# Unit 2's p in f16 by transposing transfers, unit 3 normalised on ScalarE, first loads by pair of heads, and a new order of all queues

## The chip, the cores and the metric

One core of a Trainium2 chip runs the kernel. The metric is the device time of one execution in microseconds (us). Matrix products run on TensorE (PE; its weight loads are PEld), elementwise work and reductions on VectorE (DVE), activations, copies and conversions on ScalarE (ACT), and SyncE (SP) issues nearly all transfers. GpSimd (POOL) is all but unused.

## The reference

Attention over a narrow band plus block summaries, and then a two-layer MLP. There are 4 batches, 8 heads, 768 positions and 64 columns a head; all in float32.

```python
k_sum = k.reshape(B, H, nb, 32, D).max(axis=3)       # 24 blocks of 32 keys
v_sum = v.reshape(B, H, nb, 32, D).mean(axis=3)
scores_l = scale * np.matmul(q, k.transpose(0, 1, 3, 2))
mask_l = np.abs(pos[:, None] - pos[None, :]) < 16
scores_s = scale * np.einsum('bhsd,bhnd->bhsn', q, k_sum) + np.log(32)
a = softmax(concat(where(mask_l, scores_l, -1e9), scores_s))
x = (a @ concat(v, v_sum))                            # to (3072, 512)
g = gelu(x @ w_in)                                    # w_in (512, 2048)
return g @ w_out                                      # w_out (2048, 512)
```

w_in and w_out arrive as float64 and are brought to float32 bits on VectorE.

## The kernel before

**Numbers in two halves.** Nearly every product runs in f16: an operand is split into a high part (written by ScalarE as a scaled copy in f16) and a low part (the rest, written by VectorE), and a product is three matmuls, high by high, high by low, low by high. The first six units are "wide": their scores are computed in float32 straight from q and k as loaded, with the mask put into the accumulator first (f_mask). The first three of these (u < TURNED = 3) are also "turned": p stays in float32, TensorE transposes it by matmuls with a unit matrix (p_turn, L872), ScalarE copies the result from the accumulator to pt32 (p_keep, L878), and values runs in float32 with v as loaded. From unit 3 on, p is split into p_h and p_l (s_p_hi on ScalarE, p_lo on VectorE), each is transposed by a transposing transfer on SP's queue (turn, L890) into pt_h and pt_l, which are the two halves of the buffer that pt32 covers whole, v is split too (v_hi on ScalarE, v_lo on VectorE), and values is three f16 matmuls for each tile (L915).

**Units and chunks.** A unit is 4 heads by 256 queries of one batch; there are 24. Each goes through load_q, load_v, scores (TensorE), maximum (VectorE), exponent (ScalarE, eight pieces, each with its sum), recip (VectorE), a normalisation (p_norm on VectorE, or s_norm on ScalarE, chosen for each unit), transposition, and values (TensorE). In the first batch the block means of v are computed by matmuls (sum_vt, with the matrix that load_ind brings) and copied in by ScalarE (mean_vt, s_load_vs). Then x is taken (take_hi on ScalarE, take_lo on VectorE). Two units with the same queries make a chunk of x. The MLP follows by chunks: phase1 or phase1h (half of the contraction) into gelu and g_hi (ScalarE) and g_lo (VectorE), then phase2 and store. Later chunk pairs use a scheme with seven products in place of eight (product, s_product); the last ones end with s_last and s_end.

**The start.** fetch_k brings the keys of the first batch for two pairs of heads at a time into kp0 (a row holds 768 + 96 columns for each pair), prep_k takes the block maxima of the two pairs on VectorE, and scores of a wide unit uses both (L761, four groups of 128 columns, in each first the band and then the block summaries). warm is TensorE filler. Weights follow on the same queue: fetch_wh and fetch_w_in, each with three VectorE steps to float32 bits (wh_bits, wi_bits), then wi_hi (ScalarE) and wi_lo (VectorE).

**What sets the order.** The string ORDER lists all 1648 steps, and a step's instructions go to their engines' queues in this order. Each engine takes its own queue strictly in order; it waits only for buffers and data. PSUM banks (five), the g32 slots (five), two halves of the weight staging buffer and two output tiles are rings: a step that takes a slot waits for the last reader of the slot's former tenant.

## Time and profile before

| | us |
|---|---|
| median of 3 runs | 549.82 (549.75 to 550.33) |
| the profiled execution | 549.92, of which the span is 548.1 |
| busy: TensorE | 539.9 (98%) |
| busy: VectorE, ScalarE | 452.8 (83%), 429.7 (78%) |
| moved by DMA | 74.9 MB |

The granted TensorE clock was 0.999 of full speed, a mean over the span. In the rows below a line of the timeline is start, duration, engine, source line, operation, tiles and shape, with the idle time before it and what ended that in brackets. Durations of successive instructions on one engine overlap a little, so that the next one's start tells more than the sum.

### The profile page before, as it was taken

The page shows a single profiled execution, that of the slowest core. Times are in us where ns is not written, and L with a number is a line of the kernel's source. Part 1 is how long each engine was busy: PE and PEld are TensorE (multiplying, and loading weights), DVE is VectorE, ACT ScalarE, POOL GpSimd, SP SyncE. Part 2 cuts the span into 40 slices and gives each one's busy share as a digit, 9 for nine tenths or more (in the row PEclk, how much of TensorE's full clock was granted, in tenths as well). Part 3 has the DMA queues.
Part 4 walks back from the last instruction along what each step waited for, and adds up shares of the span by engine and source line. Part 5 has one row for each costly group of instructions (what it writes and reads, how often), then busy time and mean ns, then how long its engine had stood idle before and what let it go on. Part 6 is the DMA issues. An engine that isn't in the chain of part 4 may idle for free.

```text
span 548.1 us, 14376 instructions
## 1 busy us (share of the span) xinstructions
PE 539.9 (98%) x6049; PEld 401.0 (73%) x6049; DVE 452.8 (83%) x638; ACT 429.7 (78%) x1009; POOL 0.8 (0%) x9
## 2 busy tenths in 40 slices
...
GB/s 329 408 381 195 212 242 166 172 287 198 246 224 215 174 122 157 115 200 60 121 153 109 166 80 76 105 99 118 62 69 1 1 20 1 39 2 1 11 67 59
DMA packets 73633, 74.90 MB, mean 137 GB/s; under 512 B 46944, under 2 KB 52960, under 8 KB 73568
## 3 DMA queue, kind: packets, MB, share of 16 engines
...
## 4 chain that ended last, share of the span: by engine, by line
PE 95%; DMA 2%; DVE 2%; issue 0%; ACT 0%; SPq 0%; ACTq 0%
PE bank L1017 27%; PE bank L1080 10%; PE bank L1081 10%; PE bank L1082 10%; PE bank L1194 10%; PE ps_v L923 4%; PE bank L976 4%; PE bank L989 4%; PE bank L977 4%; PE bank L978 4%; PE ps_s L793 3%; PE ps_s L1194 2%; PE ps_v L1194 2%; DMA stage<-in_w_in_dram 1%; PE ps_s L775 1%; DMA w_out_l<-in_kp_first_dram 1%
## 5 line engine op out<-in xcount | busy, mean ns | idle before, releaser
L1080 PE MATMUL bank<-w_out_h,gh 128*128 128x512 f16 x256 | 97.1, 379 | 0.0
L1081 PE MATMUL bank<-w_out_l,gh 128*128 128x512 f16 x256 | 97.0, 379 | 0.0
L1082 PE MATMUL bank<-w_out_h,gl 128*128 128x512 f16 x256 | 97.0, 379 | 0.0
L1017 PEld LDWEIGHTS <-w 128*128 128x128 f16 x640 | 62.5, 98 | 9.3
L1017 PEld LDWEIGHTS <-w_in 128*128 128x128 f16 x576 | 55.9, 98 | 9.2
L1067 DVE SCALAR_TENSOR_TENSOR gl<-g,gh 128x512 f16<-128x512 f32 x76 | 51.4, 685 | 5.9 <-ACT gh L1063 5.9
L833 ACT ACTIVATE s<-s,s_top 128x128 f32<-128x128 f32 x144 | 55.6, 390 | 0.3 <-DVE s_top L810 0.2
L1029 DVE TENSOR_TENSOR g<-bank,late 128x512 f32<-128x512 f32 x48 | 32.9, 685 | 20.4 <-PE bank L1017 9.5
L1063 ACT ACTIVATE gh<-g 128x512 f16<-128x512 f32 x76 | 45.9, 624 | 2.0 <-PE bank L1081 1.4
L1082 PEld LDWEIGHTS <-gl 128*128 128x128 f16 x256 | 25.0, 98 | 30.2
L1017 PE MATMUL bank<-x,w_in 128*128 128x256 f16 x384 | 47.1, 273 | 0.0
L1080 PEld LDWEIGHTS <-gh 128*128 128x128 f16 x256 | 25.0, 98 | 26.7
L1081 PEld LDWEIGHTS <-gh 128*128 128x128 f16 x256 | 25.1, 98 | 26.2
L1017 PE MATMUL bank<-stage,w 128*128 128x256 f16 x320 | 43.6, 273 | 0.0
L1017 PE MATMUL bank<-x,w 128*128 128x256 f16 x320 | 43.4, 273 | 0.0
L1023 ACT ACTIVATE late<-bank 128x512 f32<-128x512 f32 x48 | 28.1, 588 | 19.2 <-PE bank L1017 14.7
L976 PE MATMUL bank<-x,w_in 128*128 128x256 f16 x144 | 39.3, 273 | 0.0
L978 PE MATMUL bank<-x,w_in 128*128 128x256 f16 x144 | 39.3, 273 | 0.0
L977 PE MATMUL bank<-x,w_in 128*128 128x256 f16 x144 | 39.3, 273 | 0.0
L1049 ACT ACTIVATE g<-g 128x512 f32<-128x512 f32 x48 | 29.4, 624 | 9.1 <-DVE g L1029 9.0
L870 ACT ACTIVATE s<-s,s_rec 128x128 f32<-128x128 f32 x104 | 31.7, 390 | 2.1 <-DVE s_rec L848 2.1
L1049 ACT ACTIVATE g<-bank 128x512 f32<-128x512 f32 x48 | 27.9, 590 | 6.5 <-DVE gl L1067 2.1
...
## 6 DMA issues: line engine op xcount, KB each, us to landing
...
```

The lines of the kernel that those rows point to most:

```text
L833: nc.scalar.activation(self.s32[:, gs], score[:, ss], AF.Exp, bias=self.top[:, g : g + 1], scale=scale, accum_out=self.den[:, g : g + 1],)
L976: nc.tensor.matmul(dst, wh, xh, start=(k == 0), stop=False)
L977: nc.tensor.matmul(dst, wh, xl, start=False, stop=False)
L978: nc.tensor.matmul(dst, wl, xh, start=False, stop=(k == NCC - 1))
L1017: nc.tensor.matmul(dst, l, r[:, k], start=(first and e == 0 and k == 0 and n == 0), stop=(k == KH - 1 and n == 2), skip_group_check=True,)
L1049: nc.scalar.activation(g, h, AF.Gelu, scale=1.0 / (SC_X * SC_WI))
L1063: nc.scalar.activation(gh, two(g_slot(c, i)), AF.Copy, scale=SC_G)
L1067: nc.vector.scalar_tensor_tensor(out=gl, in0=two(g_slot(c, i)), scalar=SC_G, in1=gh, op0=ALU.mult, op1=ALU.subtract)
L1080: nc.tensor.matmul(t, gh[:, f, js], w_out_h[:, f, :], start=(n == 0), stop=False)
L1081: nc.tensor.matmul(t, gh[:, f, js], w_out_l[:, f, :], start=False, stop=False)
L1082: nc.tensor.matmul(t, gl[:, f, js], w_out_h[:, f, :], start=False, stop=(n == NFC - 1))
L1194: nc.tensor.matmul(acc[:, t * NH : (t + 1) * NH], a[:, f, js], b[:, f], start=(first and j == 0 and t == 0 and f == 0 and n == 0), stop=(f ...
```

## The change

- TURNED goes from 3 to 2: unit 2's p goes through s_p_hi, p_lo and two transposing transfers, and its v through v_hi and v_lo; its two p_turn and two p_keep fall away, and its values runs in f16.
- Unit 3 is normalised by s_norm (ScalarE) and no more by p_norm (VectorE).
- The first keys come by single pairs of heads (four fetch_kq, four prep_kq), each row with 32 columns beside the 768 and no more with 96. In the scores of a wide unit all four bands of a pair come first and then its four block summaries.
- load_v brings 96 rows and no more 128 for the units of the first batch; two memsets on POOL fill the rest with zeros once.
- ORDER is new throughout, on every engine; the steps are otherwise the same.

```diff
-TURNED = 3
+TURNED = 2
 ORDER = '''
-fetch_k 0 0, load_m16, load_q 0, fetch_k 0 1, load_eye, load_q 1, fetch_wh 6 1, fetch_wh 1 1, warm 2 9, warm 3 3,
-f_mask 0, prep_k 0 0, scores 0, maximum_p 0, prep_k 0 1, warm 0 12, f_mask 1, scores 1, load_q 2, fetch_wh 6 0,
-fetch_wh 1 0, fetch_vt 0, load_ind, fetch_w_in 4, load_q 3, load_v 0, fetch_vt 1, fetch_w_in 0, wh_bits 6 1 0,
...
+fetch_kq 1, fetch_kq 0, load_m16, load_q 0, fetch_kq 2, fetch_kq 3, fetch_wh 6 0, load_q 1, warm 0 12, prep_kq 1,
+prep_kq 0, f_mask 0, scores 0, prep_kq 2, maximum_p 0, prep_kq 3, wh_bits 6 0 0, wh_bits 6 0 1, wh_bits 6 0 2,
+f_mask 1, scores 1, warm 2 9, exponent_p 0, fetch_wh 1 0, fetch_wh 1 1, load_q 2, fetch_vt 0, load_eye,
+fetch_w_in 4, load_ind, f_mask 2, scores 2, fetch_wh 6 1, fetch_w_in 0, load_q 3, load_v 0, fetch_vt 1, load_v 1,
+fetch_w_in 2, wi_hi 6 0, maximum_p 1, wh_bits 1 0 0, recip 0, wh_bits 1 0 1, wh_bits 1 1 0, wh_bits 1 0 2,
+wh_bits 1 1 1, wi_lo 6 0, exponent_p 1, wh_bits 1 1 2, wi_hi 1 0, recip 1, wi_lo 1 0, maximum_p 2, wi_bits 4 0,
+p_norm 1, s_norm 0, wi_hi 1 1, wi_bits 4 1, p_turn 0 0, warm 1 1, p_turn 0 1, sum_vt 0, p_turn 1 1, warm 3 3,
+wh_bits 6 1 0, wi_bits 4 2, p_keep 0 0, exponent_p 2, wi_lo 1 1, recip 2, wh_bits 6 1 1, p_keep 0 1, mean_vt 0,
+wi_hi 4 0, s_load_vs 0, f_mask 3, scores 3, values 0, p_turn 1 0, sum_vt 1, s_norm 2, take_hi 0, wi_lo 4 0,
+wi_bits 0 0, wh_bits 6 1 2, wi_bits 0 1, maximum_p 3, take_lo 0, wi_bits 0 2, load_v 2, fetch_w_out 4, load_q 5,
+load_q 4, fetch_wh 7 0, s_p_hi 2, p_keep 1 1, wi_hi 4 1, p_keep 1 0, s_load_vs 2, wi_hi 0 1, mean_vt 1, wi_hi 0 0,
+s_load_vs 1, v_hi 2, phase1h 0 4 0, phase1h 0 1 0, values 1, p_lo 2, wi_bits 2 0, wi_lo 4 1, wi_bits 2 1, wi_lo 0 0,
+wi_lo 0 1, phase1h 0 6 0, phase1h 0 0 0, exponent_p 3, f_mask 4, scores 4, take_hi 1, wi_hi 6 1, v_lo 2,
+wi_bits 2 2, wo_bits 4 0, recip 3, turn 2 0, turn 2 1, s_norm 3, wi_hi 2 0, s_p_hi 3, s_load_vs 3, wi_hi 2 1,
+take_lo 1, wi_lo 6 1, wo_bits 4 1, phase1h 0 4 1, phase1h 0 0 1, values 2, phase1h 0 6 1, phase1h 0 1 1,
+fetch_wh 7 1, load_v 3, fetch_w_in 3, v_hi 3, take_hi 2, maximum_p 4, wi_lo 2 0, p_lo 3, wo_bits 4 2, wi_lo 2 1,
+wh_bits 7 0 0, phase1h 0 2 0, phase1h 0 2 1, wh_bits 7 1 0, wh_bits 7 0 1, wi_bits 3 0, take_lo 2, v_lo 3, turn 3 0,
+turn 3 1, fetch_w_in 5, exponent_p 4, f_mask 5, values 3, scores 5, gelu 0 1, take_hi 3, wi_bits 3 1, wh_bits 7 0 2,
...
-s_put 5 0 1, s_product 4 3 3, s_sum 4 0 1, s_put 4 0 1, s_last 5 0, s_last 5 1, s_end 5 0, s_end 5 1
+s_product 5 2 2, s_product 4 3 3, s_put 4 1 1, s_put 5 1 1, s_product 5 2 3, s_last 5 0, s_sum 4 0 1, s_sum 5 0 0,
+s_put 4 0 1, s_lo 5 2 4, s_product 5 3 2, s_product 5 3 1, s_product 5 3 0, s_put 5 0 0, s_end 5 0, s_lo 5 3 4,
+s_product 5 3 3, s_sum 5 0 1, s_last 5 1, s_put 5 0 1, s_end 5 1
 '''
@@
-    SP = S + 96
+    SP = S + 2 * WINDOW
@@ def setup():
+        for a in (v32[0], v_hl32[1]):
+            nc.gpsimd.memset(a[WIDE_SUM:], 0.0)
@@
+    def fetch_kq(r):
+        nc.sync.dma_start(out=kp0[:, r], in_=kp_first[r])
+
+    def prep_kq(r):
+        nc.vector.tensor_reduce(
+            out=ks32[:, r], in_=kp0[:, r, WINDOW : WINDOW + S].rearrange("p (n j) -> p n j", j=BLOCK), axis=AX.X, op=ALU.max,
+        )
@@ def load_v(self):
-            nc.sync.dma_start(out=self.v32, in_=vw[self.u].rearrange("p (n j) -> p n j", j=D))
+            rows = slice(0, P if self.b else WIDE_SUM)
+            nc.sync.dma_start(out=self.v32[rows], in_=vw[self.u, rows].rearrange("p (n j) -> p n j", j=D))
@@ def scores_wide(self):
-            for g in range(NG // 2):
-                r, t2 = g // 2, g % 2
-                for part in range(2):
+            for r in range(NR):
+                for part, t in ((part, t) for part in range(2) for t in range(CT)):
+                    g, c = r * CT // 2 + t // 2, t % 2
                     for e in range(2):
...
```

## Rows read from the trace of the kernel before

**Rows 1.** The page: TensorE, its weight loads and the other engines, busy us, share, instructions.
```profile
PE 539.9 (98%) x6049; PEld 401.0 (73%) x6049; DVE 452.8 (83%) x638; ACT 429.7 (78%) x1009; POOL 0.8 (0%) x9
```

**Rows 2.** Windows by stage: length, PE, PEld, DVE, ACT, POOL busy, clock, DMA share, GB/s.
```profile
30.00:60.00 30.00, 30.00 (x459) 26.00 (x459) 29.63 (x43) 27.54 (x70) 0.00 (x0) 1.00 0.82 279
60.00:100.00 40.00, 40.00 (x331) 28.30 (x330) 39.59 (x48) 31.15 (x61) 0.00 (x0) 1.00 0.63 205
...
500.00:550.00 50.00, 44.42 (x407) 39.57 (x405) 15.13 (x24) 11.07 (x21) 0.00 (x0) 0.97 0.11 38
```

**Rows 3.** The chain that ended last, in order of time: start, us, what (TensorE).
```profile
28.51 2.78 PE bank L597 x12
31.29 1.78 PE bank L876 x16
33.07 2.62 PE bank L989 x24
...
41.51 1.08 PE ps_v L923 x32
...
50.00 1.25 PE ps_s L775 x64
...
73.19 0.88 PE ps_v L923 x48
```

**Rows 4.** Timeline of TensorE: the first matmul of phase1 1 1.
```profile
53.38 0.27 PE L976 MATMUL bank<-x,w_in 128*128 128x256 f16 x1
```

**Rows 5.** Timeline of ScalarE, 17 to 43 us.
```profile
17.87 0.37 ACT L833 ACTIVATE s<-bank,s_top 128x128 f32<-128x128 f32 x1 [0.84 <-DVE s_top L825]
...
20.63 0.66 ACT L417 ACTIVATE late<-w 128x512 f16<-128x512 f32 x1
...
27.43 2.44 ACT L870 ACTIVATE s<-s,s_rec 128x128 f32<-128x128 f32 x8
29.77 1.05 ACT L879 ACTIVATE pt<-bank 128x512 f32<-128x512 f32 x2
...
31.73 0.37 ACT L833 ACTIVATE s<-ps_s,s_top 128x128 f32<-128x128 f32 x1
...
34.66 1.06 ACT L699 ACTIVATE v_hl<-w_out_l 24x1024 f32<-24x1024 f32 x1
...
36.80 1.13 ACT L417 ACTIVATE w_in<-w 128x512 f16<-128x512 f32 x2
...
41.60 1.06 ACT L885 ACTIVATE p_h<-s 128x1024 f16<-128x1024 f32 x1 [0.47 <-DVE s L865]
```

**Rows 6.** Timeline of VectorE: the low part of unit 3's p.
```profile
45.50 1.22 DVE L888 TENSOR_TENSOR p_l<-s,p_h 128x1024 f16<-128x1024 f32 x1
```

**Rows 7.** Timeline of SP's issues, and of ScalarE's wait for load_v 3.
```profile
43.11 2.18 SPq L892 DMA_TRANSPOSE pt<-p_h  x1
46.75 1.23 SPq L892 DMA_TRANSPOSE pt<-p_l  x1
...
47.11 1.05 ACT L699 ACTIVATE v<-w_out_l 24x1024 f32<-24x1024 f32 x1 [0.56 <-DMA v<-in_vw_dram]
```

**Rows 8.** A window in the first loads (columns as in rows 2).
```profile
10.00:12.00 2.00, 2.00 (x41) 1.10 (x42) 1.97 (x3) 2.00 (x13) 0.00 (x0) 1.00 1.05 402
```

**Rows 9.** Timeline of VectorE in the first 10 us.
```profile
5.24 1.75 DVE L556 TENSOR_REDUCE misc<-w_out_l 128x48 f32<-128x1536 f32 x1 [5.24 <-DMA w_out_l<-in_kp_first_dram]
8.28 1.23 DVE L810 TENSOR_REDUCE s_top<-ps_s 128x8 f32<-128x1024 f32 x1 [1.28 <-PE ps_s L775]
...
9.61 1.75 DVE L556 TENSOR_REDUCE misc<-w_out_l 128x48 f32<-128x1536 f32 x1
```

**Rows 10.** Timeline behind the last matmul: ScalarE, then SP.
```profile
544.51 0.66 ACT L1230 ACTIVATE ot<-bank 128x256 f32<-128x256 f32 x2 [12.51 <-PE bank L1194]
544.92 0.82 SPq L1231 DMA_DIRECT2D out_dram<-ot  x2
```

**Rows 11.** A window with one transposing transfer in it (columns as in rows 2).
```profile
68.00:71.00 3.00, 3.00 (x30) 2.68 (x28) 3.00 (x5) 3.00 (x6) 0.00 (x0) 1.00 0.39 87
```

More of the change, by code (lines that the diff above doesn't have):

```diff
@@ L81 @@
-wh_bits 6 0 2, wh_bits 1 0 0, warm 1 1, f_mask 2, scores 2, maximum_p 2, p_turn 0 1, p_turn 0 0, sum_vt 0,
-wi_hi 6 0, exponent_p 2, p_keep 0 1, mean_vt 0, p_keep 0 0, s_load_vs 0, recip 1, wh_bits 1 0 1, p_norm 1,
-wi_lo 6 0, wi_bits 4 0, wh_bits 1 0 2, wi_hi 1 0, wi_lo 6 1, wi_bits 4 1, recip 2, wi_bits 4 2, s_norm 2,
-p_turn 1 0, p_turn 1 1, f_mask 3, scores 3, values 0, p_keep 1 1, p_keep 1 0, take_hi 0, maximum_p 3, wi_lo 1 0,
-sum_vt 1, p_turn 2 1, p_turn 2 0, mean_vt 1, exponent_p 3, s_load_vs 1, wi_bits 0 0, wi_bits 0 1, take_lo 0,
@@ L86 @@
-wi_bits 0 2, phase1h 0 6 0, phase1h 0 1 0, f_mask 4, values 1, wi_bits 2 0, wi_bits 2 1, load_q 4, fetch_wh 7 1,
-recip 3, wi_hi 4 1, wi_hi 4 0, wi_hi 0 0, wi_bits 2 2, wi_hi 2 0, take_hi 1, wh_bits 7 1 0, scores 4, load_q 5,
-load_v 2, fetch_wh 7 0, fetch_w_in 3, fetch_w_out 4, p_keep 2 1, p_keep 2 0, s_load_vs 2, wi_hi 2 1, wi_lo 4 0,
-wh_bits 7 1 1, take_lo 1, phase1h 0 4 0, wi_lo 4 1, wi_lo 2 0, p_norm 3, phase1h 0 6 1, values 2, load_v 3,
-s_p_hi 3, turn 3 0, wi_lo 0 0, maximum_p 4, wi_lo 2 1, wh_bits 7 0 0, wi_bits 3 0, wh_bits 7 0 1, p_lo 3, take_hi 2,
@@ L91 @@
-wi_hi 0 1, wi_lo 0 1, wh_bits 7 0 2, wh_bits 7 1 2, turn 3 1, exponent_p 4, wo_bits 4 0, take_lo 2, s_load_vs 3,
-v_hi 3, v_lo 3, phase1h 0 4 1, phase1h 0 2 0, phase1h 0 2 1, phase1h 0 0 0, phase1h 0 1 1, f_mask 5, scores 5,
-values 3, phase1h 0 0 1, wo_bits 4 1, gelu 0 6, wi_hi 7 1, wi_lo 7 1, wi_hi 7 0, take_hi 3, take_lo 3, wo_bits 4 2,
-wi_bits 3 1, gelu 0 0, gelu 0 4, wo_hi 4, recip 4, fetch_w_in 5, fetch_kx 3 3, load_q 6, fetch_w_out 0, load_v 4,
-wi_bits 5 0, wi_bits 3 2, wi_bits 5 1, wo_lo 4, s_norm 4, g_hi 0 0, s_p_hi 4, gelu 0 1, g_hi 0 4, g_hi 0 1,
@@ L121 @@
-g_lo 2 0, take_lo 6, phase2 2 1, phase1 2 2, prep_v 3 0, q_lo 10, g_lo 2 3, phase2 2 0, t_add 1 1, p_lo 7,
-add_mask 9, g_lo 2 4, turn 7 1, k_lo 10, t_add 2 1, recip 8, s_k_hi 11, v_hi 7, v_lo 7, k_lo 11, gelu 2 7,
-store 1 0, s_norm 8, values 7, take_hi 7, scores 10, gelu 2 2, s_p_hi 8, phase2 2 5, take_lo 7, maximum 9,
-load_q 12, load_v 8, put 0 0, prep_v 3 1, q_lo 11, t_add 1 2, p_lo 8, exponent 9, s_q_hi 12, q_lo 12, recip 9,
-p_norm 9, fetch_k 2 1, turn 8 0, load_k 12, load_vs 8, turn 8 1, fetch_v 2 0, phase1 3 3, gelu 3 3, add_mask 10,
```

327 lines of the change are left out of this document (162 added, 165 removed).

## The prediction

> **What bounds the kernel now.** I read the page's busy table first, then the windows by stage, then the chain that ended last, then the first 55 us in order of time. TensorE is busy 98% of the span [rows 1], and the windows are to be read for its idle time: in the eleven from 30 us to the end it has none, but for the last one, which holds the tail (three of them stand) [rows 2]. So the end moves only by three things: TensorE work removed, TensorE idle time before about 30 us (8 us in all, with the last few in the tail), and the tail behind the last matmul. Beside it the reader is to see that TensorE is not alone: in 30 to 60 us VectorE is busy 29.63 of 30 us and ScalarE 27.54, and in 60 to 100 us VectorE 39.59 of 40 [rows 2]. The attention of the first units is a relay between the three: scores on TensorE, maxima on VectorE, exponentials on ScalarE, and back. A change that takes work from TensorE and gives it to these two in just this stage need not gain what it takes away.
>
> **TensorE's share of the change.** Unit 2 loses its two p_turn steps: 1.78 us on the chain [rows 3]. Its values become 48 f16 matmuls (0.88 us) in place of 32 records of f32 (1.08 us): 0.20 us [rows 3]. Together 1.98 us less. Everything from phase1 1 1 on is the same set of matmuls in another order, and phase1 1 1 has the same work behind it in both orders (the same ten phase1h pieces, six scores and values 0 to 3 ahead of it). So the question of the start is: when does phase1 1 1 start? Now it is at 53.38 us [rows 4].
>
> **What the others get.** ScalarE loses two p_keep (1.05 us) and gains s_norm 3 (2.34, from 27.43 to 29.77), s_p_hi 2 and v_hi 2 (1.06 each, 1024 columns a partition both): +3.4 us [rows 5]. VectorE loses p_norm 3 and gains p_lo 2 and v_lo 2, all of 1024 columns and 1.22 us, of which the next step overlaps 0.08: +1.14 us [rows 6]. SP gains two transposing transfers, of which the first pair now there took 2.18 and 1.23 us to issue [rows 7]; behind them stand fetch_wh 7 1, load_v 3 and fetch_w_in 3. On the same queue load_v 2 now waits for values 0 ahead of fetch_w_out 4, load_q 5 and 4 and fetch_wh 7 0: issued from 27 us on, their 2 MB are there by about 37 at the queue's rate [rows 8], and the first of them to be used is load_v 2, by v_hi 2 at 35: 0, with 3 us to spare. The load cuts (v of six units 512 to 384 KB, k rows of 864 to 800 columns) take 0.9 MB from a queue that moves 402 GB/s without a gap [rows 8]; they offset part of what stands earlier in the queue. The POOL memsets lie in the first microseconds, where nothing waits for POOL: 0, and at most their microsecond or two ahead of the first load's landing if VectorE were held up. The regrouped scores issue the same 32 matmuls a unit: 0; the bounds are a tenth of 1.25 us a unit either way [rows 3].
>
> **The start, laid end to end.** The first load of 864 KB lands at 5.24 us [rows 9]; at 393 KB per us [rows 8] a pair of 400 KB lands at 4.06, the second at 5.08, mask and q 0 at 5.5 and 6.15, pairs 2 and 3 at 7.2 and 8.2. A pair's maxima cost half of 1.75 us. Scores 0 then ends at 7.5, but prep_kq 2 stands ahead of maximum_p 0 on VectorE, until 8.05; now it starts at 8.28 [rows 9]. So of the 1.2 us by which the first load lands earlier, 0.25 is left for unit 0. The gain is in unit 1: maximum_p 0 (1.33) to 9.4, prep_kq 3 to 10.3, three wh_bits to 12.1, maximum_p 1 to 13.5, so exponent_p 1 starts at 13.7, against 17.87 [rows 5]. That is not a free 4.2 us, as s_norm 0 now comes behind it.
>
> From 13.7 ScalarE's queue has no gap. Up to s_load_vs 1, which values 1 needs: two exponent_p of 2.76 (17.87 to 20.63), six wi_hi of 0.52 (two, overlapped, in 1.13), s_norm 0 and 2 of 2.34, seven short ones (p_keep, take_hi, mean_vt) of about 0.53, three s_load_vs and one s_p_hi of 1.06 [rows 5]: 21.3 us, so 35.0. TensorE would be there at 33.4: f_mask 3 at about 24.0 (behind sum_vt 0, half a p_turn and three warm matmuls), then the mask about 0.75, scores 1.25, values 0 1.08, half a p_turn 0.89, sum_vt 1 2.78 and two phase1h of 1.31 [rows 3]. So **a stall of 1.6 us appears at values 1**; this is where most of the 1.98 us goes. From there both run level: values 1 and two phase1h end at 38.7, exponent_p 3 at 38.8; f_mask, scores 4, two phase1h, values 2 and four phase1h bring TensorE to 49.55; ScalarE, with the added s_norm 3 and s_p_hi, ends exponent_p 4 at 49.7 (10.9 us more). VectorE from 13.5 to v_lo 3 has thirteen steps of 1024 columns at 1.14, three maximum_p at 1.33, twenty steps of 512 columns at half the former and a little (0.6), and fourteen light ones (the shifts and recip) of about 0.43: 36.8 us [rows 6, 9], and waits once for s_p_hi 3, so v_lo 3 ends at 50.4. Then f_mask 5, values 3 and scores 5 take 2.9: phase1 1 1 at 52.6. An exponent_p also took 2.93 us (31.73 to 34.66) [rows 5]; with the mean of the two prices the four on the path are 0.3 us longer, and a tenth is left for the hand-overs between engines: 53.0. The gain of the start is 0.4 us, with bounds of 1.0 (2.76 throughout, VectorE a little earlier) and a loss of 0.6 (2.93 throughout, and 2% on the rest of a chain of 36 us).
>
> **Behind 53 us.** TensorE's queue must not run dry. Laid out likewise, VectorE ends wo_lo 0 at 76 us, and phase2 0 0 is due at 79; wi_lo 7 0 ends 1.8 us ahead of its use, wo_lo 5 1.6 us. ScalarE is behind by about 1 us at 53, and has 8.8 us of idle time in the next 40 [rows 2]. So cost 0, bounded by about 1.5 us if one of these margins fails. The stages from there to the tail are reordered with the same work on every engine, and TensorE shows no idle time in them now [rows 2]: 0 again, at most 1 us if one step is placed late.
>
> **The tail.** Both s_end 5 are now written behind s_last 5 1, and the trace shows both activations in one piece at 544.51, after 12.51 us of waiting, and two DMA issues in 0.82 us [rows 10]. In the new order s_end 5 0 stands ahead of s_last 5 1, so one activation and one issue remain: half of 0.82 plus the wait between, 0.45 us less (bounds 0, if the tile is still waited for whole, and 0.5).
>
> **A page and a row.** A transposing transfer of p_l alone, in 68 to 71 us, kept the DMA engines busy 0.39 of 3 us for 87 GB/s over 3 us, so 1.17 us for its 0.26 MB [rows 11], against 0.65 us at the 402 GB/s of loads [rows 8]. The Trainium skill (Advanced Engine Details and Errata, X-Bar Transpose (TRN2)) says that transposing DMAs are as fast as regular ones, 350 to 400 GB/s: by that unit 2's pair would be through about 0.9 us sooner than by the row. By neither does the sum change while they are hidden; the third rival's price would shrink by that much.
>
> **The sum.** The profiled execution took 549.92 us (span 548.1, 1.8 around it). 549.92 - 0.4 - 0.45 = 549.07; the median of the runs, 549.82, is 0.1 lower, so I predict **549.0 us**. About 0.2%, 1.1 us, is what a measurement of this kernel can tell from no change: faster is below 548.7, slower above 550.9.
>
> **Rivals.** (A) The forecast, 548.3 to 549.7: 0.47, of which a fifth lies below 548.7. (B) ScalarE does not bind: values 1 starts when TensorE gets there, and the 1.98 us are all gained. For it: TensorE's queue has been full from 30 us on until now [rows 2]. Against: the 21.3 us are sums of rows, and nothing in the order shortens them. 549.8 - 2.0 - 0.45 gives 547.4: 0.27. (C) The transposes turn into the wait. pt is one buffer: turn 2 cannot be issued before values 1 has read it (36.1), and it holds fetch_wh 7 1, load_v 3 and fetch_w_in 3 behind it on SP, and turn 3 must wait for values 2 (44.3). A v load issued beside a transpose at 42.7 was still waited for at 47.1 [rows 7]; so load_v 3, issued at about 40.1, lands at 44.5, and v_hi 3 is due at 45; turn 3 comes behind a 1 MB load, and its second half was issued 4.4 us ahead of its use in the kernel before, against 3.7 here. From 0.5 us of delay on, each microsecond goes into the end; with 1 MB ahead (2.6 us) the end is at 549.0 + 2.3 = 551.3: 0.16. (D) The tail gain is not there and the start comes out level, within half a microsecond of 549.8: 0.10.
>
> **Numbers.** Faster: B 0.27 and a fifth of A, 0.37. Slower: C, 0.16. Within: 0.47. The range takes in B and the lower half of C: 547.3 to 551.0.
>
> **What would show it.** Right: exponent_p 1 near 13.7, a wait of TensorE at L923 for L699 of 1 to 2 us near 35 us, phase1 1 1 near 53.0, no TensorE idle time after that, and a single activation of L1230 at the end. A wait of L923 for a transfer, or of ScalarE for load_v 3 near 45, shows C. No wait at values 1, and phase1 1 1 near 51.4, shows B. The prediction is wrong if TensorE waits in the middle of the kernel, where I counted nothing.

## The result, and the profile after

The changed kernel takes 553.18 us (median of six runs, 551.97 to 554.61) against 549.85 us of the kernel before on the same chip: a ratio of 1.0058 [1.0041, 1.0074]. It is slower by 3.3 us, where I had forecast 549.0 us in a range of 547.3 to 551.0. The profiled execution is the longest of the six, 554.61 us (span 552.8).

The busy line of the page after, beside [rows 1]; then windows (length, PE, PEld, DVE, ACT, POOL busy, clock, DMA share, GB/s), the second beside the first of [rows 2]:

```profile
PE 541.0 (98%) x6049; PEld 400.2 (72%) x6049; DVE 454.7 (82%) x641; ACT 432.9 (78%) x1017; POOL 2.7 (0%) x11
```
```profile
20.00:36.00 16.00, 15.45 (x184) 12.69 (x182) 15.13 (x23) 15.75 (x44) 0.00 (x0) 1.00 1.05 303
30.00:60.00 30.00, 26.76 (x435) 22.47 (x434) 27.09 (x38) 26.81 (x67) 0.00 (x0) 1.00 1.01 248
```

TensorE, which had no idle time in 30 to 60 us, now stands still for 3.24 us of it. The timeline of TensorE after says where: column one is the start, the bracket the idle time ahead of the instruction and what ended it. The last line answers to [rows 4].

```profile
36.95 1.15 PE L928 MATMUL ps_v<-pt,v_hl 128*64 128x64 f32 x32 [1.50 <-ACT v_hl L706]
...
52.79 0.62 PE L738 MATMUL ps_s<-misc 128*64 128x512 f16 x4 [0.81 <-ACT s L838]
...
54.20 0.22 PE L928 MATMUL ps_v<-pt,v_hl 128*64 128x64 f16 x2 [0.25 <-DMA pt<-p_l]
54.86 0.89 PE L928 MATMUL ps_v<-pt,v_hl 128*64 128x64 f16 x44 [0.44 <-DVE v_hl L903]
...
56.93 0.28 PE L981 MATMUL bank<-x,w_in 128*128 128x256 f16 x1
```

There are three places: values 1 waits for ScalarE (s_load_vs 1), scores 5 for exponent_p 4, and values 3 for turn 3 and v_lo 3. phase1 1 1 starts at 56.93 instead of 53.38 us. So I cut each run in three: the start of phase1 1 1, the time from there to the start of the last matmul ("middle"), and the tail from that start to the end of the span. In a second set of runs of the same kernel (e1) these are 57.20, 491.00 and 3.37 us, against 53.38, 490.77 and 3.99 before: +3.82, +0.23, -0.62, which is the difference of the two profiled executions, 3.43. The execution of the first set has 1.5 us more in the middle, 1.33 of it a wait of values 8 for a transposing transfer that ends at 179.7 us; e1 has none there, so it is not in every execution. The whole loss, then, lies in the first 57 us.

All kernels of the study, ratios to the kernel before, taken in the same set of runs:

| kernel | median us | ratio [95%] | phase1 1 1 | middle | tail |
|---|---|---|---|---|---|
| before | 549.85 | | 53.38 | 490.77 | 3.99 |
| after | 553.18 | 1.0058 [1.0041, 1.0074] | 56.93 | 492.52 | 3.38 |
| e1 after again | 553.35 | 1.0057 [1.0045, 1.0069] | 57.20 | 491.00 | 3.37 |
| e2 w_in 3 late | 555.65 | 1.0097 [1.0084, 1.0110] | 56.16 | 493.98 | 3.37 |
| e3 plain copies | 552.10 | 1.0035 [1.0021, 1.0049] | 55.58 | 491.43 | 3.38 |
| e4 unit 2 in f32 | 560.08 | 1.0189 [1.0172, 1.0205] | 62.06 | 491.00 | 3.33 |
| e5 v of 128 rows | 559.26 | 1.0153 [1.0135, 1.0170] | 62.97 | 491.81 | 3.37 |
| e6 before, v of 96 rows | 550.57 | 1.0006 [0.9996, 1.0016] | 53.89 | 490.77 | 4.00 |
| e7 both loads as before | 560.78 | 1.0193 [1.0179, 1.0207] | 63.44 | 492.25 | 3.37 |
| e8 v of 128 rows, sums moved | 554.82 | 1.0083 [1.0068, 1.0097] | 56.53 | 493.23 | 3.37 |
| e9 e8 with p_norm 3 | 554.37 | 1.0074 [1.0061, 1.0087] | 56.51 | 492.81 | 3.37 |
| e10 before, k by pair | 551.28 | 1.0022 [1.0008, 1.0036] | 55.16 | 490.77 | 4.43 |
| e11 before, tail swapped | 550.57 | 1.0007 [0.9998, 1.0016] | 53.38 | 492.63 | 3.45 |
| e12 after, k in two loads | 552.05 | 1.0039 [1.0025, 1.0052] | 55.70 | 491.00 | 3.32 |
| e13 all loads mended | 552.86 | 1.0043 [1.0031, 1.0056] | 55.53 | 492.90 | 3.31 |
| e14 e13, plain copies | 552.34 | 1.0033 [1.0021, 1.0045] | 54.82 | 492.10 | 3.32 |
| e15 before, tail moved | 549.33 | 0.9985 [0.9976, 0.9994] | 53.30 | 490.78 | 3.46 |
| e16 e12, plain copies | 551.51 | 1.0027 [1.0018, 1.0037] | 55.81 | 491.63 | 3.32 |
| e17 before, unit 2 alone | 553.45 | 1.0062 [1.0049, 1.0075] | 57.31 | 490.77 | 3.85 |

### The profile page after: what moved, and what is told of

It reads as the page before. It is cut to its first block, busy times and chain, and to the rows that moved or that the text cites. A ratio compares the mean times of both kernels' runs of the same rounds, so it can differ in the third digit from the quotient of the medians.

```text
span 552.8 us, 14391 instructions
## 1 busy us (share of the span) xinstructions
PE 541.0 (98%) x6049; PEld 400.2 (72%) x6049; DVE 454.7 (82%) x641; ACT 432.9 (78%) x1017; POOL 2.7 (0%) x11
## 4 chain that ended last, share of the span: by engine, by line
PE 86%; DVE 5%; DMA 4%; ACT 3%; issue 0%; SPq 0%; DVEq 0%
PE bank L1022 27%; PE bank L1085 10%; PE bank L1086 10%; PE bank L1087 10%; PE bank L1199 9%; PE ps_v L928 3%; PE bank L981 3%; PE bank L983 3%; PE bank L982 3%; PE ps_s L798 2%; PE ps_v L1199 2%; PE ps_s L1199 2%; DMA pt<-p_l 2%; DMA gl<-in_w_in_dram 2%; PE bank L994 1%; DMA w_out_l<-in_kp_first_dram 1%
## 5 line engine op out<-in xcount | busy, mean ns | idle before, releaser
L875 ACT ACTIVATE s<-s,s_rec 128x128 f32<-128x128 f32 x112 | 34.2, 391 | 1.1 <-DVE s_rec L853 1.1
L893 DVE TENSOR_TENSOR p_l<-s,p_h 128x1024 f16<-128x1024 f32 x22 | 26.8, 1219 | 9.6 <-ACT p_h L890 6.1
```

What stands on the lines that cost most here:

```text
L875: nc.scalar.activation(self.s32[:, gs], self.s32[:, gs], AF.Copy, scale=self.rec[:, g : g + 1])
```

## Experiments

**The transposes (e1 to e4).** My theory after the result was rival C: unit 2's transposes hold the loads behind them on SP's queue. SP's issues in the kernel after (start, us to issue):

```profile
38.16 1.35 SPq L897 DMA_TRANSPOSE pt<-p_h  x1
39.62 2.77 SPq L897 DMA_TRANSPOSE pt<-p_l  x1
42.45 0.58 SPq L458 DMA_DIRECT2D stage<-in_w_in_dram  x1
43.12 0.41 SPq L694 DMA_DIRECT2D v<-in_vw_dram  x1
43.59 0.42 SPq L443 DMA_DIRECT2D gl<-in_w_in_dram  x1
46.72 1.24 SPq L897 DMA_TRANSPOSE pt<-p_h  x1
48.06 4.15 SPq L897 DMA_TRANSPOSE pt<-p_l  x1
```

> The changed kernel, once more, for its spread and for which of its waits come back. In its first trace phase1 1 1 starts at 56.93 us, against 53.38 before and 53.0 forecast. Theory Q (queue): a transposing transfer that comes up behind loads stops the DMA engines, so load_v 3, fetch_w_in 3 and turn 3 are late in every execution: phase1 1 1 again between 56 and 57.5 us, VectorE again waiting 1.5 to 2.5 us for fetch_w_in 3 near 50 us, TensorE again waiting at values 3, and a median of 552.5 to 553.5. Theory D (disturbed execution): the packets of 2048 bytes that took 0.120 us instead of 0.085 between 22 and 36 us, and the engine that lags 1.6 us from 6 us on, belong to that one execution: without them phase1 1 1 starts at 54 to 55 us and the time is nearer to 551. The wait of 1.5 us at 178 us (values 8 for turn 8) comes back by Q and not by D.

The repeat stands in the table and gives the sizes above. The late start came back as Q has it; the wait at 178 us did not, which Q had wrong, and VectorE's two waits for fetch_w_in 3 were 0.8 and 1.7 us, ScalarE's for load_v 3 0.2.

e2 puts the 1 MB of fetch_w_in 3 behind turn 3.

```diff
-fetch_wh 7 1, load_v 3, fetch_w_in 3, v_hi 3, ... wi_bits 3 0, take_lo 2, ... turn 3 1, fetch_w_in 5
+fetch_wh 7 1, load_v 3, v_hi 3, ... take_lo 2, ... turn 3 1, fetch_w_in 3, fetch_w_in 5, ... wi_bits 3 0, wi_bits 3 1
```

> The changed kernel with fetch_w_in 3 (1 MB) issued behind turn 3 instead of ahead of it, and its first use wi_bits 3 0 moved behind v_lo 3 on VectorE. Theory Q: the 1 MB between the two pairs of transposes is what turn 3 and VectorE wait for: VectorE's wait of 2.04 us goes, turn 3 lands near 50 instead of 54.15, values 3 waits for no transfer, and phase1 1 1 starts 1.3 us earlier, 55.6, when f_mask 5 still waits for exponent_p 4 until 52.8: 551.9 us. Theory S (ScalarE alone sets it: exponent_p 4 ends at 52.5 and the transfers only fill its shadow): no change of more than 0.4 us.

Both forecasts were missed. phase1 1 1 is 0.8 to 1.0 us earlier, but exponent_p 1 also starts 0.7 to 1.2 us earlier here (14.62 us), long before the moved load, and from there to phase1 1 1 it is 41.5 us as in the other two (41.6 and 41.3): the move itself gained nothing. VectorE now stands at wi_bits 3 0 until the 1 MB lands at 56.67, with the x that TensorE wants behind it: a wait of 2.8 us a little later. Behind turn 3 the load is worse placed, by 2 us of the end.

e3 leaves the transposing out: the p of units 2 and 3 is copied as it lies.

```diff
+            if self.u in (2, 3):
+                nc.sync.dma_start(out=dst, in_=src)
+                return
```

> The changed kernel in which the four transposing transfers of units 2 and 3 are plain copies of the same 256 KB, from the same tiles to the same tiles; p of these two units is left untransposed, all other work is the same. Theory Q, with the transposing itself as the cause: the copies don't stop the queue, load_v 3 lands near 45 instead of 48.3, fetch_w_in 3 by 48 instead of 52.35, no wait at values 3 and none of VectorE; exponent_p 4 ends 0.7 us earlier and phase1 1 1 starts near 55.0: 551.2 us. Theory B (bytes and order alone: any 256 KB behind and ahead of these loads does the same): phase1 1 1 stays within 0.5 us of 56.9.

SP's issues in e3, and then the same stretch of the queue, in e3 and in the kernel after:

```profile
38.30 0.56 SPq L898 DMA_DIRECT2D pt<-p_h  x1
38.98 0.53 SPq L898 DMA_DIRECT2D pt<-p_l  x1
39.56 0.59 SPq L458 DMA_DIRECT2D stage<-in_w_in_dram  x1
40.65 0.85 SPq L694 DMA_DIRECT2D v<-in_vw_dram  x1
41.55 0.42 SPq L443 DMA_DIRECT2D gl<-in_w_in_dram  x1
```
```profile
38.00:44.00 6.00, 5.59 (x112) 4.53 (x107) 5.97 (x11) 5.54 (x24) 0.00 (x0) 1.00 1.06 373
40.00:44.00 4.00, 3.59 (x87) 2.78 (x86) 3.97 (x8) 3.56 (x15) 0.00 (x0) 1.00 1.07 360
```
```profile
38.00:44.00 6.00, 5.88 (x110) 4.79 (x107) 5.97 (x10) 5.84 (x25) 0.00 (x0) 1.00 1.24 182
40.00:44.00 4.00, 3.88 (x90) 3.02 (x88) 3.97 (x7) 3.85 (x15) 0.00 (x0) 1.00 1.14 85
```

With transposes the DMA engines are as busy (share 1.24 against 1.06) and move half as much; in 40 to 44 us it is 85 GB/s against 360. load_v 3 is issued 2.5 us later, lands at 48.3 instead of 47.3, and fetch_w_in 3 at 52.35 instead of 49.75. The end gains 1.2 us (1.0035 against e1's 1.0057; the two intervals overlap slightly), phase1 1 1 1.35 to 1.6, which lies between the two forecasts: rival C's mechanism is real, and it is about a third of the loss, not all of it. Of the 3.8 us by which load_v 3 lands later than the forecast 44.5, the transposing itself is 1.0. The Trainium skill (Advanced Engine Details and Errata, X-Bar Transpose (TRN2)) says that transposing DMAs are as fast as regular ones; between loads on this queue they were not.

e4 gives unit 2 back its f32 path (its values then read a v whose block means are unit 3's, as s_load_vs 3 stands ahead of values 2 in the new order).

```diff
-TURNED = 2
+TURNED = 3
-s_p_hi 2, v_hi 2, p_lo 2, v_lo 2, turn 2 0, turn 2 1
+p_turn 2 1, p_turn 2 0 (behind s_norm 2), p_keep 2 1, p_keep 2 0 (behind values 1)
```

> The changed kernel with unit 2 as it was: its p turned on TensorE (two p_turn, two p_keep) and its values in f32, all else in the new order. TensorE gets 1.98 us back, ScalarE loses s_p_hi 2 and v_hi 2 and gains two p_keep (1.1 us less), VectorE loses p_lo 2 and v_lo 2, and SP the two transposes. Theory Q: without the first pair on the queue load_v 3, fetch_w_in 3 and turn 3 are early, exponent_p 4 ends near 50.7 and phase1 1 1 starts near 54.2: 550.4 us, faster than the changed kernel although TensorE has more to do. Theory T (the work taken from TensorE is gained, whatever the queue does): 2 us slower than the changed kernel, 555.2.

560.08 us, but this settles nothing: with unit 2 in f32 one v tile serves all units but unit 1, so load_v 3 had to wait for values 2. The kernel before has this wait too, but there values 2 ends at 42.6 us; in the new order it comes later, and load_v 3 was issued at 50.35 and landed at 53.9. So what unit 2's part costs in the new order stays open. e17 below asks the question from the other side.

**The rows of v (e5 to e9).** In 20 to 36 us the queue of the changed kernel moves 303 GB/s, with its engines as busy as in [rows 8], where 402 were moved. The new v loads are 96 rows high.

```diff
-            rows = slice(0, P if self.b else WIDE_SUM)
-            nc.sync.dma_start(out=self.v32[rows], in_=vw[self.u, rows].rearrange("p (n j) -> p n j", j=D))
+            nc.sync.dma_start(out=self.v32, in_=vw[self.u].rearrange("p (n j) -> p n j", j=D))
```

> The changed kernel with the v loads of the first six units whole again: 128 rows (512 KB) instead of 96 rows (384 KB); all else, the two memsets on POOL too, stays. In both traces of the changed kernel the DMA packets between 22 and 36 us, while v 0, vt 1, v 1 and v 2 are under way, take 1.2 to 1.8 times what the same sizes take before and the queue moves about 300 GB/s, against 405 before. Theory P: the load of 96 rows does that. Then 22 to 36 us go back to about 400 GB/s although 0.4 MB more is loaded there, fetch_wh 7 0 lands near 40 instead of 42.8, turn 2 by 43 instead of 45.6, load_v 3 by 46.5 instead of 48.3, turn 3 by 52 instead of 54.2, and phase1 1 1 starts near 55.0 instead of 57: 551.3 us. Rival (the engines are out of step from the first loads on, and that slows the packets, whatever the rows): about 300 GB/s stays, and with 0.4 MB more the time is the same or up to 1 us longer, 553.2 to 554.2.

Theory P was right on the rate (410 to 413 GB/s in 24 to 28 us) and missed the time: with 128 rows the load writes the rows in which s_load_vs puts the block means, so load_v 3 waited for s_load_vs 3 (46.6) and fetch_w_in 3 landed at 56.9. (The block means of units 3 and 5 are overwritten in e5 and e7.) e6 does the reverse edit in the kernel before:

> The kernel before with one part of the change alone: v of the first six units in 96 rows instead of 128 (with the two memsets that it needs). It loads 0.77 MB less. Theory P (96 rows slow the queue): from the first v load on the queue falls from 405 to about 300 GB/s, fetch_w_out 4 lands at 44 to 46 us instead of 42.0, and load_v 2, load_q 5 and the weights behind them come 2 to 4 us later, some after they are due: 550.3 to 552.5 us. Rival (bytes count, rows don't): the queue stays at 405 and ends 1 us earlier, and as TensorE waits for no transfer there the time stays at 549.9 within 0.3.

The rate in 30 to 36 us in the kernel before and in e6, and then in 22 to 30 us in the kernel after and in e8 below, with 128 rows in the changed order:

```profile
30.00:36.00 6.00, 6.00 (x50) 5.10 (x49) 5.90 (x10) 5.90 (x22) 0.00 (x0) 1.00 1.04 406
```
```profile
30.00:36.00 6.00, 6.00 (x50) 5.04 (x48) 5.90 (x10) 5.88 (x22) 0.00 (x0) 1.00 1.05 278
```
```profile
22.00:30.00 8.00, 8.00 (x135) 6.63 (x134) 7.97 (x13) 7.87 (x30) 0.00 (x0) 1.00 1.05 282
```
```profile
22.00:30.00 8.00, 8.00 (x135) 6.60 (x134) 7.97 (x14) 7.90 (x29) 0.00 (x0) 1.00 1.03 405
```

So with 96 rows the queue as a whole is slower by about three tenths, in both orders; but the kernel before with such loads is no slower than can be measured (1.0006 [0.9996, 1.0016]). e7 takes back the row length of k too:

```diff
-    SP = S + 2 * WINDOW
+    SP = S + 96
```

> The changed kernel with whole v loads as in the run above, without the two memsets on POOL, and with the rows of k as before (864 columns, 3456 bytes, still one load for each pair of heads). In five traces with 800 columns packets of 2048 bytes take up to 0.6 to 1.2 us near 4.8 us, and one DMA engine lags the others by 0.6 to 1.8 us from q 0 on; in the kernel before none does so at that time. If the rows of 3200 bytes or the memsets do that, the lag at 6 us goes, q 0 lands at 6.3 instead of 7.2 to 8.4, exponent_p 1 starts at 13.8 to 14 instead of 14.5 to 15.8, and the time falls by a further microsecond, to 550.3; if the number of small loads issued at once does it, the lag stays and the time is that of the run above.

It has e5's wait for the block means (load_v 3 cannot start), so its time says nothing more than e5's. What it shows is in the first microseconds: q 0 still lands at 7.08, the queue still moves 283 GB/s in 4 to 6 us. Neither the row length nor the memsets delay the start. e8 is e5 with the block means placed so that no load waits for them, ahead of v_hi 3 and of v_hi 5 (unit 5's are then read after their tile has been used again); e9 is e8 with unit 3 normalised on VectorE.

```diff
-s_p_hi 3, s_load_vs 3, wi_hi 2 1, ... fetch_w_in 3, v_hi 3
+s_p_hi 3, wi_hi 2 1, ... fetch_w_in 3, s_load_vs 3, v_hi 3
```

> Whole v loads again (128 rows, 512 KB), now with s_load_vs 3 and 5 behind their unit's load (with 96 rows the two write different rows and may stand in either order; with 128 rows the load had to wait for s_load_vs 3 and came 3 us later, and its means were overwritten). So this is the clean form of the test of the 96 rows. Theory P: about 400 GB/s between 22 and 36 us, turn 2 lands near 44 instead of 45.6, load_v 3 near 46.5 instead of 48.3 to 48.6, fetch_w_in 3 near 49.5 instead of 52.4, turn 3 near 51.5 instead of 54.2; ScalarE's chain still ends exponent_p 4 near 52, and phase1 1 1 starts at 55.2 instead of 57: 551.5 us, 1.5 to 2 below the changed kernel. Rival (the time of this stage is ScalarE's alone): within 0.4 us of the changed kernel, 553.2.

```diff
-recip 3, turn 2 0, turn 2 1, s_norm 3
+recip 3, p_norm 3, turn 2 0, turn 2 1
```

> The same with unit 3 normalised on VectorE, as before (p_norm 3 behind recip 3 in place of s_norm 3): 2.45 us less on ScalarE, 1.22 more on VectorE, which waited 2 us near 50 in the changed kernel. If ScalarE's chain is what bounds the stage once the queue is at its old rate, exponent_p 4 ends 1.5 to 2.4 us earlier, near 50.3, and phase1 1 1 starts near 53.5: 549.9 us. If the queue still holds (load_v 3, turn 3), the gain is under 0.5 us: 551.2.

Both missed their forecasts of the time. With the full rate, phase1 1 1 comes only 0.4 to 0.7 us earlier: load_v 2 has to wait for values 0 (29.8 us) and load_v 3 lands at 47.6 whatever the rate was before. The end is later, since s_load_vs 4 now waits for its load and TensorE for the gelu behind it:

```profile
PE bank L976 <- ACT g L1049: 1.7, 1, 1.7
```

And e9 equals e8: in e8's order ScalarE's 2.45 us for s_norm 3 do not bind the end. For the changed kernel's own waits this was not tried.

**The first loads (e10, e12).** In e1 exponent_p 1 starts at 15.86 and after at 15.35, where I had 13.7. e10 cuts only the k loads in the kernel before, e12 joins them again in the kernel after.

```diff
-            nc.sync.dma_start(out=kp0[:, rs], in_=kp_first[rs].rearrange("r p s -> p r s"))
+            for r in (2 * g + 1 - g, 2 * g + g):
+                nc.sync.dma_start(out=kp0[:, r], in_=kp_first[r])
```

> The kernel before with one part alone: the first k loaded as four loads of a pair of heads each, in the order 1, 0, 2, 3, with the old rows of 864 columns and the old two maxima. In all traces of the changed kernel, whatever its rows of k and v and its memsets, packets of 2048 bytes are slow at 4.5 to 5 us and the last of the 16 engines lands q 0 by 0.5 to 1.8 us behind the middle one; before the kernel shows 0.17. If loading by pair does that, the lag is here too (q 0 at 6.8 to 8 instead of 6.3) and the time is 550 to 551; if it comes of the order around it (mask and q 0 between the pairs, one more load at once), the lag stays at 0.2 and the time at 549.9.

```diff
-        nc.sync.dma_start(out=kp0[:, r], in_=kp_first[r])
+        rs = slice(r, r + NR)
+        nc.sync.dma_start(out=kp0[:, rs], in_=kp_first[rs].rearrange("r p s -> p r s"))
```

> The changed kernel with one part undone: k of the first batch in two loads of two pairs each (the rows of 800 columns stay) in place of four loads of a pair. In the kernel before the four loads alone made one DMA engine lag by 2.3 us at q 0 and started phase1 1 1 1.8 us later. If they do the same here: q 0 lands near 6.3 instead of 7.2 to 8.4, with the last engine 0.2 us behind the middle one, exponent_p 1 starts near 13.9 instead of 14.5 to 15.8, phase1 1 1 near 55.8 instead of 57, and the time is 552.0, 1.3 below the changed kernel. If the wait for load_v 3, fetch_w_in 3 and turn 3 sets phase1 1 1 whatever the start: earlier exponentials, but within 0.4 us of 553.3.

VectorE's timeline in the first microseconds: the kernel after, e10, e12.

```profile
4.19 1.90 DVE L555 TENSOR_REDUCE misc<-w_out_l 128x24 f32<-128x768 f32 x2 [4.19 <-DMA w_out_l<-in_kp_first_dram]
8.92 0.95 DVE L555 TENSOR_REDUCE misc<-w_out_l 128x24 f32<-128x768 f32 x1 [2.83 <-DMA w_out_l<-in_kp_first_dram]
```
```profile
5.14 1.75 DVE L557 TENSOR_REDUCE misc<-w_out_l 128x48 f32<-128x1536 f32 x1 [5.14 <-DMA w_out_l<-in_kp_first_dram]
10.11 1.23 DVE L811 TENSOR_REDUCE s_top<-ps_s 128x8 f32<-128x1024 f32 x1 [3.22 <-PE ps_s L776]
```
```profile
5.24 1.81 DVE L552 TENSOR_REDUCE misc<-w_out_l 128x24 f32<-128x768 f32 x2 [5.24 <-DMA w_out_l<-in_kp_first_dram]
8.61 0.95 DVE L552 TENSOR_REDUCE misc<-w_out_l 128x24 f32<-128x768 f32 x1 [1.55 <-DMA w_out_l<-in_kp_first_dram]
```

The first pair comes earlier, as planned, and the third comes at 8.92, not 7.2. The trace's DMA records show how: a load is done when the last of the 16 engines has its share, and with loads by pair one engine lags. In e10 q 0 is done on the middle engine at 6.24 and on the last at 8.59; in the kernel before 6.11 and 6.28. The queue as a whole is slower in e10 than before:

```profile
4.00:6.00 2.00, 2.00 (x6) 0.64 (x4) 0.86 (x1) 0.00 (x0) 0.00 (x0) 1.00 0.91 301
```
```profile
4.00:6.00 2.00, 1.87 (x10) 0.64 (x8) 0.76 (x1) 0.00 (x0) 0.00 (x0) 1.00 1.04 403
```

In all ten traces with loads by pair the last engine is 0.54 to 2.34 us behind the middle one at q 0 (1.63 in the kernel after); in the nine with loads of two pairs it is 0.16 to 0.41. The price is 1.2 us of the end in e10; joining the loads gives back 1.0 in the changed kernel (e12's 1.0039 against 1.0058, intervals that touch; phase1 1 1 at 55.70). e12 met its forecast of the time, but by luck: exponent_p 1 comes at 15.04, 0.3 to 0.8 us earlier and not near 13.9, since two loads of two pairs bring the third pair only at 8.6. The rest of the gain lies behind it, where load_v 3 lands at 46.98 instead of 48.31. The Trainium skill (Perfetto Trace Analysis, DMA Optimizations) says that splitting DMAs may allow some to start sooner; the first load landed sooner here (4.04 us in e10, 5.22 before), and the kernel was later for it.

**The tail (e11, e15).** e11 swaps two steps of the kernel before. The change has them in the same order, but with other steps between s_end 5 0 and s_last 5 1. e15 moves s_last 5 0 and s_end 5 0 ahead of s_product 4 3 3.

```diff
-s_put 4 0 1, s_last 5 0, s_last 5 1, s_end 5 0, s_end 5 1
+s_put 4 0 1, s_last 5 0, s_end 5 0, s_last 5 1, s_end 5 1
```

> The kernel before with its last steps in the new order alone: s_end 5 0 ahead of s_last 5 1. From the last matmul to the end it was 3.98 us before and is 3.37 to 3.38 in the traces of the changed kernel, against a forecast of 0.45 less. If that is the order of these steps: 0.6 us less, 549.3. If it comes of something else in the new order: 549.9.

```diff
-s_put 5 0 1, s_product 4 3 3, s_sum 4 0 1, s_put 4 0 1, s_last 5 0, s_last 5 1, s_end 5 0, s_end 5 1
+s_put 5 0 1, s_last 5 0, s_end 5 0, s_product 4 3 3, s_sum 4 0 1, s_put 4 0 1, s_last 5 1, s_end 5 1
```

> The kernel before with s_last 5 0 and s_end 5 0 moved ahead of s_product 4 3 3 (its four passes and s_last 5 1 then lie between the read of the bank's first half and the next write of it). With s_end 5 0 just ahead of s_last 5 1 the tail was 0.54 us shorter but TensorE waited 0.59 us for that read. If that wait is all that ate the gain: no wait here, the tail at 3.4 to 3.45, 549.3 against 549.9, which would be below both kernels. If not, 549.9.

The end of TensorE's timeline in e11, then in e15:

```profile
543.50 1.47 PE L1190 MATMUL bank<-pt,w_in 128*128 128x256 f16 x12 [0.52 <-ACT ot L1226]
```
```profile
541.56 1.47 PE L1190 MATMUL bank<-pt,w_in 128*128 128x256 f16 x12
```

Both tails are 0.5 us shorter. But in e11 s_last 5 1 must wait 0.52 us for ScalarE to read the first half of its bank, and nothing is left (its execution also shows 0.76 us of waiting for a transposing transfer that ends at 118 us); with other matmuls in between the wait is gone. e15 takes 549.33 us against 549.98 in its set of runs, 0.9985 [0.9976, 0.9994]: a small gain, and the one version here that beats both kernels.

**Together (e13, e14, e16).** e13 is e12 with v of 128 rows, no memsets, the block means of units 2 and 3 just ahead of v_hi 2 and 3, fetch_w_in 3 behind fetch_w_in 2, s_load_vs 4 behind gelu 1 4, and load_v 5 behind v_lo 4; e14 is e13 with e3's plain copies; e16 is e12 with them.

```diff
-fetch_w_in 2, ... s_load_vs 2, wi_hi 0 1, mean_vt 1, wi_hi 0 0, s_load_vs 1, v_hi 2
+fetch_w_in 2, fetch_w_in 3, ... wi_hi 0 1, mean_vt 1, wi_hi 0 0, s_load_vs 1, s_load_vs 2, v_hi 2
```

> The changed kernel with its transfers mended and its engines' work and the transposes kept: k in two loads, whole v loads (each s_load_vs behind its load, load_v 5 as soon as v_lo 4 is through), and fetch_w_in 3 issued behind fetch_w_in 2, where the queue has room when it runs at 400 GB/s. If transfers are what the forecast missed, and the transposes are no more than 256 KB each: exponent_p 1 near 13.9, no wait of VectorE for fetch_w_in 3, turn 3 by 50.5, phase1 1 1 near 53.5, the 53.0 of the forecast within a microsecond: 549.9 us. If the transposes hold the queue by themselves: turn 2 lands near 43.5, load_v 3 near 47, phase1 1 1 near 54.8, 551.2.

> The same with plain copies in place of the four transposing transfers of units 2 and 3 (p of these units stays untransposed). What is left is the relay of the engines. If the forecast summed it rightly, phase1 1 1 starts at 53.0 to 53.3 and the time is 549.4 to 549.7; the difference to the run above is what the transposing costs, 0 to 0.4 us by the forecast, 1.3 by the plain copies in the changed kernel. If phase1 1 1 stays above 54, the sum of ScalarE's and VectorE's rows was too small too.

> The changed kernel with both single causes undone together: k in two loads of two pairs, and plain copies in place of the transposes of units 2 and 3 (p of these two stays untransposed). Each alone gave 1.3 us. If they are two causes: phase1 1 1 near 54.5 and 550.8 us. If both work through the same wait (load_v 3 behind turn 2 on the queue), the second gives less: 55.2 and 551.5.

The end of the start in e14, TensorE:

```profile
51.93 0.62 PE L732 MATMUL ps_s<-misc 128*64 128x512 f16 x4
52.69 0.95 PE L925 MATMUL ps_v<-pt,v_hl 128*64 128x64 f16 x48
54.82 0.28 PE L978 MATMUL bank<-x,w_in 128*128 128x256 f16 x1
```

Here no wait for a transfer is left at the end of the start (load_v 3 lands at 44.58), and phase1 1 1 is still 1.4 us later than before; e14's last branch came true. e13 missed both its forecasts (phase1 1 1 at 55.53). In both TensorE waits again for gelu near 72 us, 1.11 and 0.94 us, so the moved steps of units 4 and 5 are not free. In e16 both repairs together give 1.7 us (1.0027 against 1.0058), e3 and e12 alone 1.2 and 1.0; 551.51 is what the second branch said, but whether less than the sum is real, the intervals leave open. 1.5 us of loss remain. e16's profiled execution is the second longest of its nine, so its cut in the table says little of sizes.

**Unit 2 alone (e17).** The kernel before, its loads untouched, with only unit 2's p in f16.

```diff
-TURNED = 3
+TURNED = 2
-p_turn 2 1, p_turn 2 0, p_keep 2 1, p_keep 2 0
+s_p_hi 2 (behind s_norm 2), p_lo 2 (take_lo 0), turn 2 0, turn 2 1 (fetch_w_out 4), v_hi 2 (s_load_vs 2), v_lo 2, load_v 3 (take_lo 1)
-phase1h 0 6 1, values 2, load_v 3, s_p_hi 3, turn 3 0, ... wh_bits 7 1 2, turn 3 1
+phase1h 0 6 1, s_p_hi 3, ... wh_bits 7 1 2, phase1h 0 4 1, phase1h 0 2 0, phase1h 0 2 1, values 2, turn 3 0, turn 3 1
-p_lo 3, take_hi 2
+exponent_p 4, take_hi 2
```

> The kernel before with unit 2's part alone: p and v of unit 2 in f16 (s_p_hi 2, p_lo 2, v_hi 2, v_lo 2), turned by two transposing transfers behind fetch_w_out 4, values 2 three pieces of phase1h later, load_v 3 ahead of it; first loads, unit 3's p_norm and all else as before. TensorE has 1.98 us less to do, ScalarE 1.07 more, VectorE 2.3 more. If VectorE's and ScalarE's relay binds these 20 us (VectorE ends v_lo 3 at 50.86 and values 3 starts at 51.18 before): v_lo 3 ends 2.3 us later, near 53.2, TensorE waits for it, phase1 1 1 starts near 55.4 and the time is 551.9. If their margins hide it, the 1.98 us are gained: 51.4 and 547.9.

TensorE's longest waits in its 36 to 58 us, from the views of waits and time:

```profile
PE bank L985 <- DVE w_in L417: 2.9, 2, 1.5
```
```profile
44.03 2.79 PE L985 MATMUL bank<-x,w_in 128*128 128x256 f16 x24 [1.44 <-DVE w_in L417]
48.30 1.27 PE L985 MATMUL bank<-x,w_in 128*128 128x256 f16 x10 [1.48 <-DVE w_in L417]
```

phase1 1 1 is 3.9 us late although TensorE has 2 us less to do. It waits 2.9 us for weights that VectorE makes, and before that 1.6 us, by 33.3 us, for x, which ScalarE and VectorE write. The wait for v_lo 3 that I had named did not appear, and both forecasts were missed. In the order of the kernel before the part costs 3.4 us of the end; another order around it may cost less, and was not tried.

## Why the prediction was wrong, point by point

**Right.** The bound: all that moved lies in the start, in the tail and in a few waits. The middle is 491.00 us against 490.77, 0.23 where I counted 0. My sign of being wrong, a wait in the middle, did show in the first set's execution (values 8), but not in e1. TensorE's saving of 1.98 us was not realised, as I had argued against rival B (0.27). The stall at values 1 was forecast as 1.6 us, ending at 35.0, by ScalarE's queue; it was 1.50 us, ending at 36.95, by just that line. In e1 it was only 0.7, so that the size came out is partly luck. ScalarE's sum from exponent_p 1 to s_load_vs 1 was 21.3 us forecast and 21.54 measured (15.35 to the end of this line, 36.89):

```profile
35.84 1.05 ACT L706 ACTIVATE v_hl<-w_out_l 24x1024 f32<-24x1024 f32 x1
```

The tail gave 0.61 (e1 0.62) where I had 0.45, with this one activation and issue left in place of the two of [rows 10]:

```profile
549.76 0.38 ACT L1235 ACTIVATE ot<-bank 128x256 f32<-128x256 f32 x1 [6.11 <-PE bank L1199]
```

**The step that failed first: when the loads land.** I laid the first loads end to end at 393 KB per us, so "pairs 2 and 3 at 7.2 and 8.2" and exponent_p 1 at 13.7. Pair 2 was used at 8.92, exponent_p 1 came at 15.35. The steps between were right: from the third maxima to exponent_p 1 it is 6.4 us in the kernel after, in e12 (8.61 to 15.04) and in e5, and 6.5 in the forecast. The middle one of the 16 DMA engines kept to the forecast within 0.5 us: it had its share of the first pairs at 3.62 and 4.66 (forecast 4.06 and 5.08), of q 0 at 6.18 (6.15), of pairs 2 and 3 at 7.35 and 8.35 (7.2 and 8.2). The last engine had its own at 7.81 for q 0 and at 8.89 and 9.87 for pairs 2 and 3. So the step that failed is the landing: the rate of [rows 8] was a rate of whole loads over all engines, and a load ends with its slowest. That costs 1.65 us at exponent_p 1. It varies: in the nine executions with these first steps the third maxima start between 7.51 (e5, exponent_p 1 at 13.94, near the forecast) and 9.44 (e1). That the cutting brings the lag, e10 and e12 show; why it does, stays open.

**The second: the transposes.** Rival C (0.16, 551.3 us) had the mechanism. It was mis-sized: load_v 3 was to land at 44.5 and landed at 48.3, since turn 2 was issued at 38.16 (not 36.1), and since I had priced a pair at twice the 1.17 us of a transfer that stood alone on the queue [rows 11]. Between loads p_l alone took 2.77 us to issue and landed 6.0 us after its issue began (45.59); as a plain copy (e3) it took 4.4. No single repair brings load_v 3 near 44.5 (e3 47.3, e12 46.98, e8 47.6); e14, with all of them and fetch_w_in 3 out of the way, does (44.58). In the kernel after, ScalarE waited for load_v 3, and VectorE for fetch_w_in 3 ahead of v_lo 3:

```profile
48.41 1.06 ACT L900 ACTIVATE v_hl<-v 128x1024 f16<-128x1024 f32 x1 [0.70 <-DMA v<-in_vw_dram]
```
```profile
52.38 0.69 DVE L404 TENSOR_SCALAR w<-gl 128x1024 int32<-128x1024 int32 x1 [2.04 <-DMA gl<-in_w_in_dram]
53.59 1.22 DVE L903 SCALAR_TENSOR_TENSOR v_hl<-v,v_hl 128x1024 f16<-128x1024 f32 x1
```

My condition for C (half a microsecond of delay) was passed several times over. I gave the price of a row taken on an empty queue to transfers that stand among loads, with no upper bound for that case: this is what left the range too short.

**The sum of the error.** 53.0 was forecast for phase1 1 1, 56.93 measured: 1.65 from the landing of pair 2, 0.25 from ScalarE's sum, 1.15 up to the end of exponent_p 4 (15.85 in place of 14.7, 0.70 of it the wait for load_v 3), and 0.9 behind it (4.2 in place of 3.3), where values 3 waits for turn 3 and v_lo 3. With loads joined and transposing taken out (e14) the sums are nearer: exponent_p 4 ends 36.6 us after exponent_p 1, where I had 36.0, and 3.1 us remain where I had 3.3. So there the relay was sized to within 2%, and even then 54.8 is later than the 53.4 of before: two loads of two pairs bring the third pair at 8.6, and with 15.07 in place of 13.7 for exponent_p 1 the start is 1.4 us late, more than the forecast gain of 0.4 us. No run shows the loss of the changed kernel undone: the two repairs together (e16) leave 1.5 us of it, and that these are the later start of exponent_p 1 is read from e14's sums and not tested.

**Wrong in sign.** I counted the smaller v loads as an offset; they move fewer bytes, at 278 to 282 in place of 405 GB/s. Whole loads brought phase1 1 1 forward by 0.4 to 0.7 us (e8), and e14, which has them and the moves that go with them, has it 1.0 us ahead of e16. Nor was there "3 us to spare" for load_v 2: it landed at 36.69 and was used at 36.92, and fetch_wh 7 0 landed at 42.87, where I had all by about 37. What the smaller loads do bring is that a v load need not wait for the block means of its tile (e5).

**A term that was not there: the clock.** In 12 of the 13 traces of the new order (all but e2) TensorE's granted clock stands at 0.50, the lower of its two levels, for 3.41 us within the first 25 us; in none of the six of the old order does it. In the kernel after this is 12.96 to 16.37, behind 2 us (10 to 12) in which TensorE was busy 0.07:

```profile
14.00:16.00 2.00, 2.00 (x7) 0.79 (x6) 1.93 (x7) 1.37 (x7) 0.00 (x0) 0.50 1.06 407
```

There it cost nothing, since TensorE waits for ScalarE soon after (0.26 us at 19.10, then at values 1). In e1 it comes at 21.2 and falls on sum_vt 0, which takes 3.50 us in place of 2.75, and ScalarE waits for it:

```profile
26.64 0.38 ACT L610 ACTIVATE w_out_l<-bank 24x256 f32<-24x256 f32 x1 [0.78 <-PE bank L603]
```

No run isolates what brings it down: e2 waits 1.83 us at the same place and keeps the full clock.
